# Masks' products ahead of the decays' in the score and maximum groups; the last output tile in two column halves

## The chip, the cores and the metric

One core of one Trainium2 chip runs the kernel. The metric is device time in microseconds (us), the median of several executions. One execution was also taken by the hardware profiler; its span runs from the program's first to its last instruction. Engines are named as the profile names them: PE is the matrix engine (TensorE) and PEld its weight loads, DVE is VectorE, ACT is ScalarE, POOL is GpSimd, SP is SyncE.

## The reference, cut to what matters

```python
B, H, S, D = 8, 8, 576, 64                     # attention
scores = q @ k.T / sqrt(D)
cum = cumsum(log(clip(f, 1e-4, 1)), -1)
scores = where(causal, -1e9, scores + cum[..., :, None] - cum[..., None, :])
attn = exp(scores - max(scores)); attn /= sum(attn) + 1e-9
x = (attn @ v).transpose(0, 2, 1, 3).reshape(4608, 512)
# mixture of 8 experts, one for each row
e = argmax(x @ w_gate)
out[row] = gate[row] * sigmoid(x @ w_output_gate)[row, e] * (relu(x @ w1[e]) @ w2[e])
```

Weights are float32: w1 is 8 x 512 x 1024, w2 is 8 x 1024 x 512.

## The kernel before, in words

**Attention.** The 64 heads are worked off two at a time, in 32 units. The head dimension is 64, so head 0 of a unit lies on partitions 0 to 63 and head 1 on 64 to 127, and `heads` (line 301) issues each product for head 0 and at once for head 1; the two use different rows of the matrix engine's array. A score in PSUM is a sum of products into the same columns, a *group*: Q times K (float32 for the scores proper, the upper halves as bf16 for the estimate of the maxima); the *decay* product, whose stationary operand comes from `Ek` or `Eq` and whose rows hold the cumulated log decays, the ones and, in the last row of `Eq`, the row maxima; and, for blocks on the diagonal, two *mask* products of 64 columns with the constant `pick` as stationary operand, which add -8e9 above the diagonal. `score` (line 410) makes the groups of the scores, `block` (line 319, inside `maxsteps`) those of the maxima. In the profile `sc` and `rs` are the scores' PSUM tiles, `mx` the maxima's, `sc<-qk` is the float32 product, `sc<-Eq,Ek` and `mx<-Ek,Eq` are the decays' and `negt,pick` and `negm,pick` the masks'. All products of both kinds are issued by one line, 305, and have that line in the profile. A float32 product is executed in two passes, each with a weight load of its own.

ScalarE exponentiates the scores (line 426), GpSimd forms the low half of the result (line 428), the products with V follow (lines 499 to 512), DVE takes the maxima (line 331). What is issued at which step is written out by hand: each unit has six steps, `OFF` gives the step of every kind of work and `OFF["order"]` the order inside a step, and each engine executes in that order. The maxima run about two units ahead of the scores. On the matrix engine a unit gives, among other things: the bank of 512 score columns, maxima groups of 384 and 128 columns, products with V, then the off-diagonal 64 score columns (two products, no mask), the maxima group of 256, the score group of 448, the small rest scores (`rs`) and rest maxima, the score groups of 320 and 192, the maxima group of 512, products with V. For the last two units there are no maxima groups left. Between products on 64 rows and products on 128 rows the array changes its shape.

**Experts.** Rows are routed while attention still runs; then, expert by expert, rows are gathered by an indirect DMA, multiplied by w1 (line 1057, in high and low 16-bit parts), and `down_sum` (line 1077) multiplies 128 rows by w2: 24 products of 512 columns into one PSUM tile `y`. `down_out` (line 1090) scales `y` on ScalarE into `ys` (line 1093), and `put_rows` (line 1096) writes the rows with an indirect DMA issued by GpSimd (line 1097). The loop at line 1250 takes the experts in turn; the last one has 512 rows, four tiles. After it stands a loop (line 1292) over overflow slots.

Of the kernel before, what the change touches and what calls it, by code (L numbers as in the profile page):

```python
# [9 lines left out]
F32 = mybir.dt.float32  # L10
# [3 lines left out]
I32 = mybir.dt.int32  # L14
AF = mybir.ActivationFunctionType
ALU = mybir.AluOpType
# [4 lines left out]
P = 128  # L21
B, H, S, D = 8, 8, 576, 64
NT = B * S
DM = H * D
# [53 lines left out]
def _attn_moe(ctx, tc, qk, vm, f, wg, w1, w2, out):  # L78
    nc = tc.nc
# [45 lines left out]
    def rows(i):  # L125
        return slice(i * D, (i + 1) * D)
# [74 lines left out]
    order = actx.enter_context(ExitStack())  # L201
# [7 lines left out]
    pick, negm, negt = [cp.tile([P, 2, P], BF16, name=n) for n in ("pick", "negm", "negt")]  # L209
# [97 lines left out]
    def maxsteps(u):  # L307

        t = st[u]
        Ku, Qu = upper(t["K"]), upper(t["Q"])  # L310
        nR = t["nR"] = a.tile([P, NW], F32, name="nR", bufs=3)
        w = HU * NC
        nW = nR[:, 0:w].rearrange("p (i c) -> p i c", i=HU)

        def few(x, i, sl):

            return x[i * D:(i + 1) * D - 1, sl]

        def block(m, o, c):
            n = (c + 1) * P  # L320
            q = slice(c * P, n)
            return [(lambda i: m[i][:, o:o + n], lambda i: Qu[rows(i), q], lambda i: Ku[rows(i), 0:n], True, False),
                    (lambda i: m[i][:, o:o + n], lambda i: few(t["Eq"], i, q), lambda i: few(t["Ek"], i, slice(0, n)),
                     False, False),
                    (lambda i: m[i][:, o + n - P:o + n - D], lambda i: pick[rows(i), 0],
                     lambda i: negm[rows(i), 0, 0:D], False, False),
                    (lambda i: m[i][:, o + n - D:o + n], lambda i: pick[rows(i), 1], lambda i: negm[rows(i), 1, D:],
                     False, True)]

        def red(o, x):  # L330
            nc.vector.tensor_reduce(o, x, axis=AX.X, op=ALU.max, negate=True)  # L331

        def mtile():
            return ps.tile([P, 2, 512], F32, name="mx", bufs=1)

        def banks(step):

            name = ("mx av sc".split(), "av mx sc".split(), "av mx mx".split())[u][step] if u < 3 else "mx"
            if name == "mx":
                m = mtile()  # L340
                return [m[:, i] for i in range(HU)], [(slice(0, HU), m)]
            ms = [ps.tile([P, 512], F32, name=name, bufs={"av": 2, "sc": 3}[name]) for _ in range(HU)]
            return ms, [(i, m) for i, m in enumerate(ms)]

        def reds(parts, c, a, b):
            for i, m in parts:
                red(nW[:, i, c] if isinstance(i, slice) else nW[:, i, c:c + 1], m[..., a:b])

        def full():
            m, parts = banks(0)  # L350
            heads(block(m, 0, 3))
            yield
            reds(parts, 3, 0, 512)

        def mixed():
            m, parts = banks(1)
            heads(block(m, 0, 2))
            heads(block(m, 384, 0))
            yield
            reds(parts, 2, 0, 384)  # L360
            reds(parts, 0, 384, 512)

        def second():
            m, parts = banks(2)
            heads(block(m, 0, 1))
            yield
            reds(parts, 1, 0, 256)

        def rest():
            m = mtile().rearrange("p b n -> p (b n)")[:, 0:S]  # L370
            q = slice(SM, S)
            for sl in (slice(0, SM), q):
                own = sl is q
                heads([(lambda i: m[rows(i), sl], lambda i: Qu[rows(i), q], lambda i: Ku[rows(i), sl], True, False),
                       (lambda i: m[rows(i), sl], lambda i: few(t["Eq"], i, q), lambda i: few(t["Ek"], i, sl),
                        False, not own)])
            heads([(lambda i: m[rows(i), q], lambda i: pick[rows(i), 0, 0:SR], lambda i: negm[rows(i), 0, 0:SR],
                    False, True)])
            yield
            red(nR[:, w:w + 1], m)  # L380

        return {0: full(), 2: mixed(), 4: second(), 5: rest()}
# [27 lines left out]
    def score(u, dst, kc, q0, n):  # L410

        t = st[u]
        m = min(P, S - kc * P)
        ks, qs = slice(kc * P, kc * P + m), slice(q0, q0 + n)
        diag = q0 == kc * P
        out = [(dst, lambda i: t["K"][rows(i), ks], lambda i: t["Q"][rows(i), qs], True, False),
               (dst, lambda i: t["Ek"][rows(i), ks], lambda i: t["Eq"][rows(i), qs], False, not diag)]
        if diag:
            out += [(lambda i: dst(i)[:, 0:D], lambda i: pick[rows(i), 0, 0:m], lambda i: negt[rows(i), 0, 0:D], False,
                     m == D)]  # L420
        if diag and m > D:
            out += [(lambda i: dst(i)[:, D:P], lambda i: pick[rows(i), 1], lambda i: negt[rows(i), 1, D:], False, True)]
        return out

    def expo(f32, lo, src, eng=None):
        nc.scalar.activation(out=f32, in_=src, func=AF.Exp, scale=0.125)  # L426
# [338 lines left out]
    NF = FF // P  # L765
# [23 lines left out]
    W2, W2r = [], {}  # L789
# [199 lines left out]
    m2 = ctx.enter_context(tc.tile_pool(name="m2", bufs=2, reuse_waits="tile"))  # L989
    m1 = ctx.enter_context(tc.tile_pool(name="m1", bufs=1, reuse_waits="tile"))  # L990
    pm = ctx.enter_context(tc.tile_pool(name="pm", bufs=2, space=PSUM, reuse_waits="tile"))
# [96 lines left out]
    written = []  # L1088
# [37 lines left out]
    def down_narrow(w2s, x, h, t, rest):  # L1126
# [5 lines left out]
                narrow_out(x, t, ys, y, n, p0)  # L1132
        put_rows(ys[0:64 if rest <= 64 else 96], x, t)

    def down(w2s, x, h, t0, t1, looped=False):
        for t in range(t0, t1):
            down_out(x, down_sum(w2s, h, t), t, looped)
# [8 lines left out]
    x = st["early"]  # L1146

    with tc.manual_schedule(engines=ENGINES):
# [15 lines left out]
        h = hidden()  # L1164
# [85 lines left out]
        for n in range(len(CAPS) + 1):  # L1250
# [18 lines left out]
            for t in range(nt):  # L1269
                gather_turn(x1, t)  # L1270
            for t in range(tiles):
                rest = cap - t * P
                y = down_sum(W2, h, t) if rest > 96 else None
                if nx:
                    for fc in range(2 * t, min(2 * t + 2, NF)):
                        W1n.append(load_w1(nx["w1"], fc, W1r))
                        if fc + AHEAD < NF:
                            W1r.append(fetch_w1(m2, nx["w1"], fc + AHEAD, 8))
                    if t == 3:
                        W2r = [fetch_w2(nx["w2"], fc) for fc in range(AHEAD)]  # L1280
                if y is None:
                    down_narrow(W2, x, h, t, rest)
                else:
                    down_out(x, y, t)
                if n == 0 and t == 3:
                    ncum = overflow_slots()
                if n == 2 and t == 0:
                    nsl = nc.values_load(ncum, min_val=0, max_val=(NT - min(CAPS)) // P + E)
# [75 lines left out]
```

## Time and profile before

| | |
|---|---|
| median of 3 runs | 745.55 us (745.58, 741.25, 745.55) |
| profiled execution, its own time | 742.9 us |
| its span, first to last instruction | 741.2 us |
| mean granted clock of PE | 0.996 |
| PE busy | 718.6 us, 97% of the span |
| POOL, DVE, ACT busy | 455.9, 370.0, 336.6 us |
| last matmul starts | 733.02 us |

1.7 us of the profiled execution lie around its span. A busy PE is a PE with a matmul in its pipeline, whose end is modelled; how fast products follow each other is read from their starts.

### The profile page before, as it was taken

The page shows a single profiled execution, that of the slowest core. Times are in us where ns is not written, and L with a number is a line of the kernel's source. Part 1 is how long each engine was busy: PE and PEld are TensorE (multiplying, and loading weights), DVE is VectorE, ACT ScalarE, POOL GpSimd, SP SyncE. Part 2 cuts the span into 40 slices and gives each one's busy share as a digit, 9 for nine tenths or more (in the row PEclk, how much of TensorE's full clock was granted, in tenths as well). Part 3 has the DMA queues.
Part 4 walks back from the last instruction along what each step waited for, and adds up shares of the span by engine and source line. Part 5 has one row for each costly group of instructions (what it writes and reads, how often), then busy time and mean ns, then how long its engine had stood idle before and what let it go on. Part 6 is the DMA issues. An engine that isn't in the chain of part 4 may idle for free. (4 is left out here: it accounts for less than half of the span.)

```text
span 741.2 us, 21637 instructions
## 1 busy us (share of the span) xinstructions
PE 718.6 (97%) x8871; PEld 444.3 (60%) x8890; DVE 370.0 (50%) x853; ACT 336.6 (45%) x761; POOL 455.9 (62%) x513
## 2 busy tenths in 40 slices
PE   4999999999999999999999999999999999999995
PEld 2677776777777777787576645545445444454442
DVE  7567687888879797777513305203133042040220
ACT  4456666575757665564412333423424324243221
POOL 8769698898989898871422552543634726545321
PEclk9999999999999999999999999999999999999998
DMA  4435766776866465248473574554744936547101
GB/s 154 159 114 156 169 159 142 186 181 155 192 178 174 146 172 163 50 98 219 104 211 104 138 193 154 127 197 142 172 137 144 256 96 144 201 136 235 61 15 40
DMA packets 119431, 110.69 MB, mean 149 GB/s; under 512 B 82654, under 2 KB 92062, under 8 KB 119328
## 3 DMA queue, kind: packets, MB, share of 16 engines
q1 hardware_dynamic: 108566, 71.50, 37.5%
q10 hardware_dynamic: 4618, 18.88, 8.5%
q0 software_dynamic: 6144, 18.88, 7.8%
q8 instruction: 71, 1.16, 0.6%
q14 instruction: 32, 0.26, 0.1%
HBM read 72.47 MB, written 19.49 MB: 124 GB/s over the span
## 5 line engine op out<-in xcount | busy, mean ns | idle before, releaser
L428 POOL TENSOR_TENSOR plo<-p 128x512 f16<-128x512 f32 x182 | 191.1, 1066 | 37.5 <-ACT p L426 35.5
L1057 PE MATMUL hp<-xT,w1h 128*128 128x512 f16 (+2 forms) x960 | 175.2, 298 | 0.0
L331 DVE TENSOR_REDUCE nR<-mx 128x2 f32<-128x1024 f32 (+4 forms) x154 | 121.4, 805 | 48.3 <-PE mx L305 46.6
L426 ACT ACTIVATE p<-sc 128x512 f32<-128x512 f32 x192 | 111.6, 594 | 72.8 <-PE sc L305 66.1
L305 PE MATMUL sc<-qk 64*128 64x448 f32 (+5 forms) x644 | 129.2, 474 | 0.0
L1067 DVE SCALAR_TENSOR_TENSOR hl<-hp,hh 128x512 f16<-128x512 f32 (+2 forms) x120 | 54.1, 484 | 139.6 <-ACT hh L1066 132.0
L1057 PE MATMUL hp<-xT,w1l 128*128 128x512 f16 (+2 forms) x480 | 111.7, 298 | 0.0
L1057 PEld LDWEIGHTS <-w1h 128*128 128x128 f16 x960 | 74.2, 97 | 56.7 <-issue 1.9
L1066 ACT ACTIVATE hh<-hp 128x512 f16<-128x512 f32 (+2 forms) x120 | 47.0, 433 | 132.6 <-PE hp L1057 128.7
L1085 PE MATMUL y<-w2h,hl 128*128 128x512 f16 x280 | 106.1, 379 | 1.0
L1083 PE MATMUL y<-w2h,hh 128*128 128x512 f16 x280 | 106.1, 379 | 0.0
L1084 PE MATMUL y<-w2l,hh 128*128 128x512 bf16 x261 | 98.9, 379 | 0.0
L1001 POOL TENSOR_TENSOR w2l<-w2r,w2h 128x512 bf16<-128x512 f32 x28 | 32.3, 1152 | 96.7 <-ACT w2h L1000 96.7
L305 PEld LDWEIGHTS <-pick 64*128 64x128 bf16 (+1 forms) x1152 | 58.9, 97 | 49.8 <-issue 27.6
L1097 POOL DMA_INDIRECT out_dram<-ys,idsr x29 | 28.8, 992 | 72.9 <-ACT ys L1093 48.0
L499 PE MATMUL av<-Vs,p 128*128 128x65 f16 x640 | 65.8, 193 | 1.3 <-ACT xr L546 1.3
L500 PE MATMUL av<-Vs,p 128*128 128x64 bf16 x640 | 65.7, 195 | 0.0
L305 PE MATMUL mx<-qk 64*128 64x512 bf16 (+3 forms) x372 | 57.8, 303 | 7.8 <-DMA qk<-in_qk_dram 5.5
L501 PE MATMUL av<-Vs,plo 128*128 128x65 f16 x640 | 65.4, 192 | 0.0
L500 PEld LDWEIGHTS <-p 128*128 128x128 bf16 x640 | 59.4, 97 | 1.4 <-issue 1.4
L499 PEld LDWEIGHTS <-p 128*128 128x128 bf16 x640 | 59.1, 97 | 1.3
L501 PEld LDWEIGHTS <-plo 128*128 128x128 f16 x640 | 59.4, 99 | 0.0
(226 smaller groups left out, 1390.1 us busy)
## 6 DMA issues: line engine op xcount, KB each, us to landing
qk<-in_qk_dram ACTq DMA_DIRECT2D x31, 576.0 KB
w1r<-in_w_dram SPq DMA_DIRECT2D x64, 256.0 KB
w2r<-in_w_dram SPq DMA_DIRECT2D x64, 256.0 KB
v<-in_vm_dram SPq DMA_DIRECT2D x15, 576.0 KB
xbuf<-x SPq DMA_DIRECT2D x16, 512.0 KB
Eq<-mts SPq DMA_DIRECT2D x64, 0.1 KB
xbuf<-x SPq DMA_DIRECT2D x16, 64.0 KB
xT<-x SPq DMA_TRANSPOSE x62
```

Of the source, the lines that this page charges most:

```text
L305: nc.tensor.matmul(dst(i), w(i), x(i), start=start, stop=stop)
L331: nc.vector.tensor_reduce(o, x, axis=AX.X, op=ALU.max, negate=True)
L426: nc.scalar.activation(out=f32, in_=src, func=AF.Exp, scale=0.125)
L428: eng.tensor_tensor(lo, f32, upper(f32), op=ALU.subtract)
L499: nc.tensor.matmul(dst, ph, vv[:, 0:W], start=kc == 0, stop=False)
L500: nc.tensor.matmul(dst[:, 0:D], ph, vv[:, W:].bitcast(BF16), start=False, stop=False)
L501: nc.tensor.matmul(dst, pl, vv[:, 0:W], start=False, stop=kc == qc)
L1057: nc.tensor.matmul(m[:, 0:c1 - c0], w[:, k], x, start=k == 0 and i == 0, stop=k == ND - 1 and i == 2)
L1067: nc.vector.scalar_tensor_tensor(hl[:, fc, sl], m, 0.0, hh[:, fc, sl], op0=ALU.max, op1=ALU.subtract)
L1083: nc.tensor.matmul(y, hh[:, fc, sl], wh, start=fc == 0, stop=False)
L1084: nc.tensor.matmul(y, hh[:, fc, sl], wl, start=False, stop=False)
L1085: nc.tensor.matmul(y, hl[:, fc, sl], wh, start=False, stop=fc == NF - 1)
```

## The change

In `score` and `block` the mask products are issued right behind Q times K and the decay product last; it now closes the group. Only the maxima of the first unit (u = 0) keep the old order. The rest maxima (`rest`) are not touched. Score groups without a mask stay as they were.

The last tile of the last expert goes through a new function, `down_halves`: the 24 products of 512 columns become 48 of 256, first all for columns 0 to 255 and then all for 256 to 511, each half with its own PSUM tile, its own scaling on ScalarE and its own indirect DMA. The output is seen as 9,216 rows of 256; the row numbers, 2 x id and 2 x id + 1, are made by two small DVE operations.

```diff
--- before.py
+++ after.py
@@ -316,16 +316,21 @@
 
             return x[i * D:(i + 1) * D - 1, sl]
 
+        def order(adds):
+
+            adds = adds if u else adds[2:] + adds[:2]
+            return [(*x, False, x is adds[-1]) for x in adds]
+
         def block(m, o, c):
             n = (c + 1) * P
             q = slice(c * P, n)
             return [(lambda i: m[i][:, o:o + n], lambda i: Qu[rows(i), q], lambda i: Ku[rows(i), 0:n], True, False),
-                    (lambda i: m[i][:, o:o + n], lambda i: few(t["Eq"], i, q), lambda i: few(t["Ek"], i, slice(0, n)),
-                     False, False),
-                    (lambda i: m[i][:, o + n - P:o + n - D], lambda i: pick[rows(i), 0],
-                     lambda i: negm[rows(i), 0, 0:D], False, False),
-                    (lambda i: m[i][:, o + n - D:o + n], lambda i: pick[rows(i), 1], lambda i: negm[rows(i), 1, D:],
-                     False, True)]
+                    *order([(lambda i: m[i][:, o + n - P:o + n - D], lambda i: pick[rows(i), 0],
+                             lambda i: negm[rows(i), 0, 0:D]),
+                            (lambda i: m[i][:, o + n - D:o + n], lambda i: pick[rows(i), 1],
+                             lambda i: negm[rows(i), 1, D:]),
+                            (lambda i: m[i][:, o:o + n], lambda i: few(t["Eq"], i, q),
+                             lambda i: few(t["Ek"], i, slice(0, n)))])]
 
         def red(o, x):
             nc.vector.tensor_reduce(o, x, axis=AX.X, op=ALU.max, negate=True)
@@ -413,14 +418,13 @@
         m = min(P, S - kc * P)
         ks, qs = slice(kc * P, kc * P + m), slice(q0, q0 + n)
         diag = q0 == kc * P
-        out = [(dst, lambda i: t["K"][rows(i), ks], lambda i: t["Q"][rows(i), qs], True, False),
-               (dst, lambda i: t["Ek"][rows(i), ks], lambda i: t["Eq"][rows(i), qs], False, not diag)]
+        out = [(dst, lambda i: t["K"][rows(i), ks], lambda i: t["Q"][rows(i), qs], True, False)]
         if diag:
             out += [(lambda i: dst(i)[:, 0:D], lambda i: pick[rows(i), 0, 0:m], lambda i: negt[rows(i), 0, 0:D], False,
-                     m == D)]
+                     False)]
         if diag and m > D:
-            out += [(lambda i: dst(i)[:, D:P], lambda i: pick[rows(i), 1], lambda i: negt[rows(i), 1, D:], False, True)]
-        return out
+            out += [(lambda i: dst(i)[:, D:P], lambda i: pick[rows(i), 1], lambda i: negt[rows(i), 1, D:], False, False)]
+        return out + [(dst, lambda i: t["Ek"][rows(i), ks], lambda i: t["Eq"][rows(i), qs], False, True)]
 
     def expo(f32, lo, src, eng=None):
         nc.scalar.activation(out=f32, in_=src, func=AF.Exp, scale=0.125)
@@ -1131,6 +1135,32 @@
                 y = narrow_sum(w2s, h, t * P + p0, n)
                 narrow_out(x, t, ys, y, n, p0)
         put_rows(ys[0:64 if rest <= 64 else 96], x, t)
+
+    def down_halves(w2s, x, h, t):
+
+        hh, hl = h
+        sl = slice(t * P, (t + 1) * P)
+        n = DM // 2
+        pos = m1.tile([P, 2], I32, name="pos")
+        for j in range(2):
+            nc.vector.tensor_scalar(pos[:, j:j + 1], x[0][:, t, 0:1], 2.0, float(j), op0=ALU.mult, op1=ALU.add)
+        for j in range(2):
+            y = pm.tile([P, DM], F32, name="y", bufs=2)
+            cols = slice(j * n, (j + 1) * n)
+            for fc in range(NF):
+                wh, wl = w2s[fc]
+                nc.tensor.matmul(y[:, 0:n], hh[:, fc, sl], wh[:, cols], start=fc == 0, stop=False)
+                nc.tensor.matmul(y[:, 0:n], hh[:, fc, sl], wl[:, cols], start=False, stop=False)
+                nc.tensor.matmul(y[:, 0:n], hl[:, fc, sl], wh[:, cols], start=False, stop=fc == NF - 1)
+            ys = m2.tile([P, DM], F32, name="ys", bufs=3)[:, 0:n]
+            nc.scalar.activation(out=ys, in_=y[:, 0:n], func=AF.Copy, scale=x[0][:, t, 1:2].bitcast(F32))
+            ins = nc.gpsimd.indirect_dma_start(
+                out=out.rearrange("t (h d) -> (t h) d", h=2), in_=ys, in_offset=None,
+                out_offset=bass.IndirectOffsetOnAxis(ap=pos[:, j:j + 1], axis=0),
+                bounds_check=2 * NT - 1, oob_is_err=False)
+            for other in written:
+                tc.declare_no_dep(ins.ins, other.ins, reason="distinct rows or columns")
+            written.append(ins)
 
     def down(w2s, x, h, t0, t1, looped=False):
         for t in range(t0, t1):
@@ -1269,6 +1299,9 @@
             for t in range(nt):
                 gather_turn(x1, t)
             for t in range(tiles):
+                if nx is None and t == tiles - 1:
+                    down_halves(W2, x, h, t)
+                    continue
                 rest = cap - t * P
                 y = down_sum(W2, h, t) if rest > 96 else None
                 if nx:
```

## Rows read from the trace of the kernel before

**Rows 1.** Waits of PE, whole span: waiter, releaser, us in total, times, longest.
```profile
PE mx L305 <- DVE nR L331: 1.7, 2, 0.9
```

**Rows 2.** Busy us by stretch: length, PE, PEld, DVE, ACT, POOL; PEclk, DMA share, GB/s.
```profile
100.00:200.00 100.00, 99.11 (x1990) 74.04 (x1987) 84.17 (x194) 64.79 (x156) 88.79 (x98) 1.00 0.73 173
```

**Rows 3.** Timeline, 301.1 to 306 us: start, duration, engine, operation, count.
```profile
301.63 0.28 PE L305 MATMUL mx<-Ek,Eq 63*128 63x256 f16 x2
...
301.74 0.23 PE L305 MATMUL mx<-negm,pick 64*128 64x64 bf16 x4
301.78 0.30 PEld L305 LDWEIGHTS sc<-qk 64*128 64x128 f32 x4
301.80 1.00 PE L305 MATMUL sc<-qk 64*128 64x448 f32 x4
...
302.64 0.35 PE L305 MATMUL sc<-Eq,Ek 64*128 64x448 f16 x2
302.64 0.29 PEld L305 LDWEIGHTS <-pick 64*128 64x128 bf16 x4 [0.28 <-issue]
...
304.53 0.30 PE L305 MATMUL sc<-Eq,Ek 64*128 64x320 f16 x2
...
304.67 0.23 PE L305 MATMUL sc<-negt,pick 64*128 64x64 bf16 x4
...
304.69 0.31 PEld L305 LDWEIGHTS sc<-qk 64*128 64x128 f32 x4
304.72 0.57 PE L305 MATMUL sc<-qk 64*128 64x192 f32 x4
...
305.13 0.25 PE L305 MATMUL sc<-Eq,Ek 64*128 64x192 f16 x2
...
305.27 0.40 PE L305 MATMUL mx<-qk 64*128 64x512 bf16 x2
...
305.50 0.39 PE L305 MATMUL mx<-Ek,Eq 63*128 63x512 f16 x2
...
305.72 0.23 PE L305 MATMUL mx<-negm,pick 64*128 64x64 bf16 x4
```

**Rows 4.** The same timeline in narrow windows: a float32 product's second pass alone.
```profile
301.89 0.19 PEld L305 LDWEIGHTS sc<-qk 64*128 64x128 f32 x2
...
302.26 0.54 PE L305 MATMUL sc<-qk 64*128 64x448 f32 x2
```

**Rows 5.** Groups of weight loads by form: busy us, mean ns, idle before.
```profile
L305 PEld LDWEIGHTS sc<-qk 64*128 64x128 f32 x640 | 50.0, 186 | 4.7
...
L305 PEld LDWEIGHTS <-Ek 64*128 64x128 f16 x320 | 18.5, 106 | 17.1 <-issue 14.8
```

**Rows 6.** Timeline, 726 to 745 us: the last tile.
```profile
733.02 0.38 PE L1085 MATMUL y<-w2h,hl 128*128 128x512 f16 x1
733.49 0.69 ACT L1093 ACTIVATE ys<-y,idsr 128x512 f32<-128x512 f32 x1 [4.54 <-PEq L1292]
734.45 0.97 POOL L1097 DMA_INDIRECT out_dram<-ys,idsr  x1 [4.26 <-POOLq L1292]
```

**Rows 7.** Timeline of PE around 384 us: products of 256 columns.
```profile
383.75 0.38 PE L1057 MATMUL hp<-xT,w1h 128*128 128x256 f16 x2
```

**Rows 8.** Groups of instructions of ACT by form, 400 to 742 us.
```profile
L1066 ACT ACTIVATE hh<-hp 128x512 f16<-128x512 f32 x48 | 28.7, 597 | 101.1 <-PE hp L1057 99.3 <-issue 1.7
...
L1066 ACT ACTIVATE hh<-hp 128x256 f16<-128x256 f32 x7 | 2.6, 378 | 0.0
```

**Rows 9.** DMAs from 724 to 727 us, one output tile: packets, MB, share.
```profile
q0 software_dynamic: 80, 0.26, 23.2%
...
out_dram<-ys,idsr POOLq DMA_INDIRECT x1, 2.7
```

**Rows 10.** DMAs from 693 to 696 us, a smaller output tile: last number us to landing.
```profile
q0 software_dynamic: 48, 0.07, 10.1%
...
out_dram<-ys,idsr POOLq DMA_INDIRECT x1, 2.3
```

## The prediction

> **What bounds the kernel now.** I read the page's busy shares first, then the waits of PE, then the stretches, then the timeline of one unit, and the tail last. PE is busy 97% of the span, but a busy PE is only one with a product in flight, so the waits decide: on another engine's work PE waits 1.7 us in the whole run [rows 1]; its longer ones are for the first loads, at the very start. In a typical stretch of attention PE is busy 99.11 of 100 us while POOL has 88.79, DVE 84.17 and ACT 64.79 [rows 2]. So attention lasts as long as PE's products take to follow each other, and what counts is the distance between starts. At the end the bound changes: after the last matmul's start at 733.02 comes a chain of ScalarE, GpSimd and one output DMA [rows 6], and 741.2 - 733.02 = 8.2 us of the span hold no further product.
>
> **How the starts follow each other.** The score product in float32 is the one place where PE loses time to a weight load. Take the bank of 448: its two passes start at 301.80 and 302.26 and the next product at 302.64 [rows 3, 4]. The passes stream the same columns, yet the first takes 0.46 us and the second 0.38. The first pass's load started at 301.78, 0.02 before its pass, because the products ahead of it were masks: four of 64 columns, begun at 301.74 and over in 0.06 [rows 3]. The second pass's load started at 301.89, 0.37 ahead [rows 4], and costs nothing. The float32 load is also the long one, 186 ns [rows 5]. So a float32 product that follows masks loses 0.08 us. The bank of 192 fits: 304.72 to 305.13 is 0.41 for both passes [rows 3]; 0.38 x 192/448 = 0.16 for a pass without loss leaves 0.25 for the first, a loss of 0.09, with its load 0.03 ahead.
>
> **Part 1, the float32 product after the decay.** With the decay last, a product of 256 columns (maxima) stands before the 448 and one of 320 columns before the 192. Those pairs now take 0.11 (301.63 to 301.74) and 0.14 (304.53 to 304.67) [rows 3]. A load starts with the product before it: the masks' load at 302.64 with the decay at 302.64 [rows 3]. So the float32 load would be 0.11 and 0.14 ahead instead of 0.02 and 0.03. Is that enough? A lead of 0.02 loses 0.08, so a load that must be some 0.10 ahead is the estimate (0.02 + 0.08, and 0.03 + 0.09 for the other); 0.11 and 0.14 reach it or miss by about 0.01. I take 0.08 gained at each place. How many: the 192 follows the 320 in all 32 units; the 448 follows a maxima group in 30 (the maxima run two units ahead, so the last two units have none). The other float32 products don't gain: the 512, the 64, the 320 and the rest scores follow a change of the array's shape or an unmasked group. Sum: 62 x 0.08 = **-5.0 us**. Bounds: 0 if nothing is hidden, 62 x 0.09 = -5.6 if all is.
>
> **Part 2, the decay after the masks.** Its 16-bit load now gets only the short masks as cover, where before it had the long product Q times K. No row shows a decay after masks. The nearest is a bf16 product after masks: the maxima's Q times K of 512 columns after the masks takes 0.23 (305.27 to 305.50), the decay of 512 columns after a long product 0.22 (305.50 to 305.72) [rows 3]. So 0.01, and by the rounding between 0 and 0.02. Groups that get it: 4 score groups in 32 units and 4 maxima groups in 31, 252 in all. Three maxima groups a unit lose it in turn, since their Q times K now follows a decay instead of masks: 3 x 31 = 93. Net 159 x 0.005 (half of the 0.01 read, as shorter groups have less to lose) = **+0.8 us**. Upper bound by another row: the decay's load takes 106 ns [rows 5] and the masks cover about 0.03 of it; if all the rest were exposed, 252 x 0.07 = 18 us. The row after masks is much nearer to this case, so I take the small value. The masks' own loads move from beside the decay to beside Q times K, which is as long or longer: nothing. The order within PSUM adds no wait, as the group is complete at the same place in the queue and ACT and DVE read it only when its last product is done.
>
> One rule speaks against part 1. The second pass's load ran from 301.89 while the first pass, on the same rows of the array, streamed until 302.26 [rows 3, 4]: a load overlaps a product of its own rows here. The Trainium skill (TensorE: Matmul & The Clock Gate, The mechanism) says that weight loads overlap with matmuls in flight only when their row group differs; by that, each head's float32 load would wait for its own head's decay, part 1 would give 0, and what stays of parts 1 and 2 is +0.8.
>
> **Part 3, waits.** The decay of the scores needs the row maxima by DMA; later in the group it can only wait less. At the start PE still waits for DVE's maxima, so a gain there is lost; I put 0 on it, within 0.2 either way.
>
> **Part 4, the tail.** PE: two products of 256 columns last 0.38 together [rows 7], as long as one of 512 [rows 6], so 48 take what 24 took; 0, at most +0.1. The first half's ACT, POOL and DMA work lies beside the second half's products (24 of them, at the 0.11 that 256 columns take [rows 3], are 2.6 us), and its 0.97 on POOL is over before the second half asks. The two operations for row numbers run on DVE, which has nothing else then; uncovered they would cost some tenths. On the path stands the second half's chain. ACT: 512 columns take 597 ns and 256 take 378 in the nearest form [rows 8], so -0.22 of its 0.69. POOL: as many rows, 0.97 again, 0. The DMA: a tile of 0.26 MB lands 2.7 us after its issue and one of 0.07 MB after 2.3 [rows 9, 10]; 0.13 MB less is 0.4 x 0.13/0.19 = -0.27. But those smaller ones had fewer rows, not shorter ones, so between 0 and -0.4; I take -0.25. What follows the landing stays. Sum **-0.45**, from -0.1 to -0.7.
>
> **The sum.** -5.0 + 0.8 - 0.45 = -4.65 us. Against the profiled execution 742.9 - 4.65 = 738.3. Its median of runs lies 2.65 higher, so **740.9 us** there. The bounds of the terms give -6.3 (-5.6 + 0 - 0.7) to -2.5 (-4.0, if such a lead hides only four fifths, + 159 x 0.01 - 0.1), or 739.2 to 743.1. The runs of before lie 4.3 us apart, 0.6%; 1% (7.5 us) is about what a measurement of this kernel can tell from no change.
>
> **The rivals.** *A: the float32 load isn't hidden*, because it can't start beside a decay, or the first pass is slow for another reason (a change from bf16 to float32, say). For it: no row has a float32 product after a long one with a full-length load ahead. Against it: the second passes. It leaves +0.8 - 0.45 = +0.35: 745.9. *B, slower: the decay's load is laid bare behind the short masks.* Its place is the 252 groups, its price up to 0.07 each. It decides from (5.0 + 0.45)/252 = 0.022 us a group on; at 0.04 it is +10.1 - 5.45 = +4.6, 750.2, at its full price 758. Against it: Q times K after masks, at 0.01. *C: PE becomes faster and another engine ends later.* POOL has 88.79 of 100 us [rows 2]; a unit of about 10 us (32 fill some 330 us of the timeline) would shrink by 0.16, 1.6%, which leaves POOL under 91%. If local jams ate half of the gain: -2.1 - 0.45, 743.0. That the change does nothing at all can't be: the order of products is fixed by hand.
>
> **How the numbers follow.** Chances: the forecast 0.70, A 0.13, C 0.12, B 0.05. The forecast's own range is 739.2 to 743.1; with the spread of the runs, whose lowest lies 4.3 below the median, down to 736.5, and up to 745.5, which takes in C. A and B, 0.18, stay mostly outside. Faster by over 1% would need more than every term's bound, or a median of low runs: 0.14. Slower by over 1% is B at the better part of its price: 0.03. The rest, 0.83, is within 1%.
>
> **What would show it.** Right: in the new timeline the float32 loads of 448 and 192 start with the decay before them, 0.11 to 0.14 ahead, and the first pass takes as long as the second; 192 then takes 0.33 instead of 0.41 and 448 takes 0.76 instead of 0.84. The decay of 512 columns after masks takes 0.23. A unit is some 0.14 shorter, and the first products of the experts come 4 us earlier. In the tail the last ACT operation takes 0.47 and the last DMA lands some 0.25 sooner after its issue. Wrong: first passes still 0.08 longer than second ones (A), decays 0.03 or more longer than their columns (B), new waits of PE for ACT or DVE (C), or a last DMA whose shorter rows take as long as before.

## The result, and the profile after

The changed kernel takes 735.19 us, median of four runs (734.88 to 735.32); the kernel before takes 744.37 in the four runs beside them. The ratio is 0.988, interval 0.985 to 0.992. The prediction was 740.9 with a range of 736.5 to 745.5: right in direction, too small, and 1.3 us outside the range. In two further sets, on two chips, the same kernel had ratios of 0.991 (0.989 to 0.993) and 0.992 (0.989 to 0.995); its 16 runs together have the median 735.9 and go from 733.8 to 740.3. That the first four lie within 0.4 us is not borne out by the twelve others.

The profiled execution took 735.31 us, its span 733.6, 7.6 less than before's 741.2. I read it in the same order. First the waits of PE (waiter, releaser, us in total, times, longest) and the stretch of 100 us in attention:

```profile
PE mx L305 <- DVE nR L336: 1.6, 2, 1.1
...
PE hp L1061 <- DMA xT<-xg: 0.4, 1, 0.4
...
100.00:200.00 100.00, 99.22 (x2017) 72.17 (x2016) 86.25 (x194) 65.86 (x162) 90.90 (x98) 1.00 0.76 176
```

This view names no new wait for ACT or DVE in the units [rows 1], but it counts only time in which no product is in flight; the starts say more (Part 2 below). POOL is at 90.90 instead of 88.79 [rows 2], as rival C had worked out, and still not the bound. One wait in it is new: the first product of the experts waits 0.4 us for the gathered rows. Then the timeline of one unit:

```profile
294.97 0.22 PE L305 MATMUL mx<-negm,pick 64*128 64x64 bf16 x4
...
295.02 0.28 PE L305 MATMUL mx<-Ek,Eq 63*128 63x256 f16 x2
295.02 0.31 PEld L305 LDWEIGHTS sc<-qk 64*128 64x128 f32 x4
295.13 0.92 PE L305 MATMUL sc<-qk 64*128 64x448 f32 x4
...
295.89 0.22 PE L305 MATMUL sc<-negt,pick 64*128 64x64 bf16 x4
...
297.91 0.30 PE L305 MATMUL sc<-Eq,Ek 64*128 64x320 f16 x2
297.92 0.33 PEld L305 LDWEIGHTS sc<-qk 64*128 64x128 f32 x4
298.05 0.49 PE L305 MATMUL sc<-qk 64*128 64x192 f32 x4
...
298.38 0.23 PE L305 MATMUL sc<-negt,pick 64*128 64x64 bf16 x4
...
301.77 0.38 PE L305 MATMUL sc<-Eq,Ek 64*128 64x512 f16 x2
...
301.99 0.34 PE L305 MATMUL mx<-qk 64*128 64x384 bf16 x2
```

The float32 load of the 448 starts with the decay, at 295.02, 0.11 ahead of its product; that of the 192 0.13 ahead. From start to start the 448 takes 295.13 to 295.89, 0.76, where it took 0.84; the 192 takes 298.05 to 298.38, 0.33, where it took 0.41 [rows 3]. The decay of 512 columns after masks takes 0.22 (301.77 to 301.99), as it did after a long product [rows 3].

The two traces can be compared at four points that both kernels pass. The transpose `mt` that opens the third unit starts at 31.24 before and 28.51 after; that of the last unit at 317.89 and 310.96. First the rows of before, then those of after:

```profile
31.24 0.23 PE L393 MATMUL mt<-identh,mh 128*128 128x128 f16 x1
317.89 0.23 PE L393 MATMUL mt<-identh,mh 128*128 128x128 f16 x1
```
```profile
28.51 0.23 PE L398 MATMUL mt<-identh,mh 128*128 128x128 f16 x1
310.96 0.23 PE L398 MATMUL mt<-identh,mh 128*128 128x128 f16 x1
```

| up to | after minus before, us | gained since the row above |
|---|---|---|
| third unit's transpose | 28.51 - 31.24 = -2.73 | -2.73 |
| last unit's transpose | 310.96 - 317.89 = -6.93 | -4.20 |
| start of the last matmul | 726.41 - 733.02 = -6.61 | +0.32 |
| end of the span | 733.6 - 741.2 = -7.6 | -1.0 |

The second line, for 29 of the 32 units, is near what parts 1 and 2 forecast for all, -5.0 + 0.8. The first line was forecast as 0, the last as -0.45. So the result has two questions: what happened in the first 30 us, and what at the end. The start first; two rows of the trace before, then two of after (same products, same place in the queue):

```profile
18.36 0.63 PE L305 MATMUL mx<-qk 64*64 64x512 bf16 x2 [0.86 <-DVE nR L331]
18.79 0.63 PE L305 MATMUL mx<-Ek,Eq 63*64 63x512 f16 x2
```
```profile
17.79 0.41 PE L305 MATMUL mx<-qk 64*64 64x512 bf16 x2 [1.10 <-DVE nR L336]
18.04 0.38 PE L305 MATMUL mx<-Ek,Eq 63*64 63x512 f16 x2
```

From one start to the next 512 columns take 0.43 us before and 0.25 after: TensorE still ran at 1.2 GHz in the one trace and already at 2.4 in the other. By the granted clock on record, which the starts of such products bear out, it rose for good at 22.4 us in before's trace and at 15.1 in after's. I had read no row of before's start for its clock.

### The profile page after: what moved, and what is told of

Read it like the earlier page. It is cut to its first block, busy times and chain, and to the rows that moved or that the text cites. A ratio compares the mean times of both kernels' runs of the same rounds, so it can differ in the third digit from the quotient of the medians.

```text
span 733.6 us, 21711 instructions
## 1 busy us (share of the span) xinstructions
PE 712.3 (97%) x8914; PEld 436.2 (59%) x8914; DVE 373.7 (51%) x855; ACT 337.2 (46%) x762; POOL 458.3 (62%) x514
## 5 line engine op out<-in xcount | busy, mean ns | idle before, releaser
L305 PE MATMUL sc<-qk 64*128 64x448 f32 (+5 forms) x644 | 122.9, 455 | 0.0
L1088 PE MATMUL y<-w2l,hh 128*128 128x512 bf16 x272 | 103.1, 379 | 0.0
L1089 PE MATMUL y<-w2h,hl 128*128 128x512 f16 x272 | 103.1, 379 | 0.0
L1087 PE MATMUL y<-w2h,hh 128*128 128x512 f16 x272 | 103.1, 379 | 0.0
```

The source lines that it names most:

```text
L305: nc.tensor.matmul(dst(i), w(i), x(i), start=start, stop=stop)
L1087: nc.tensor.matmul(y, hh[:, fc, sl], wh, start=fc == 0, stop=False)
L1088: nc.tensor.matmul(y, hh[:, fc, sl], wl, start=False, stop=False)
L1089: nc.tensor.matmul(y, hl[:, fc, sl], wh, start=False, stop=fc == NF - 1)
```

## The experiments

Every kernel was timed in five rounds beside the kernel before. "Diff" is the mean of its runs minus the mean of the runs of the kernel before on that chip, with the standard error of its own runs; "start" is the third unit's transpose, "units" the time from there to the last unit's (before 286.65, after 282.45), "end" the time from the last matmul's start to the end of the span (before 8.18, after 7.20).

| run | ratio (interval) | diff | start | units | end |
|---|---|---|---|---|---|
| after_again | 0.991 (0.989-0.993) | -7.2 ± 0.7 | 28.39 | 281.63 | 6.94 |
| after_third | 0.992 (0.989-0.995) | -5.8 ± 0.8 | 31.23 | 282.31 | 6.98 |
| before_look | 1.000 (0.999-1.002) | +0.2 ± 0.5 | 30.47 | 286.40 | 8.09 |
| unit1_only | 0.999 (0.997-1.001) | -0.8 ± 0.4 | 31.11 | 285.87 | 8.14 |
| old_start | 0.992 (0.990-0.994) | -6.2 ± 0.5 | 30.21 | 281.64 | 7.23 |
| old_start_again | 0.992 (0.990-0.994) | -6.0 ± 0.4 | 30.47 | 282.64 | 7.31 |
| scores_only | 0.996 (0.994-0.998) | -3.6 ± 0.6 | 28.82 | 283.56 | 8.24 |
| maxima_only | 0.996 (0.994-0.998) | -2.9 ± 0.6 | 28.65 | 286.78 | 8.48 |
| halves_only | 1.000 (0.998-1.001) | -0.8 ± 0.5 | 30.59 | 285.87 | 6.96 |
| split_decay | 0.996 (0.994-0.998) | -3.0 ± 0.5 | 31.44 | 285.71 | 6.90 |
| two_places | 0.993 (0.991-0.995) | -6.1 ± 0.9 | 28.43 | 281.98 | 7.01 |
| whole_tile | 0.994 (0.991-0.996) | -5.4 ± 0.7 | 28.50 | 281.93 | 8.01 |

In about half of the traces PE pauses once (in two of them twice) in the units, with 0.4 to 2.85 us from one start to the next, mostly between 110 and 140 us and mostly with nothing in the profile that it waits for. maxima_only's is the longest, 2.85, so that its units took 283.9 without it. after's has 0.7. before's costs 0.9, and there the profile does name a wait, the one for the row maxima:

```profile
PE sc L305 <- DMA Eq<-mts: 0.6, 1, 0.6
```

Among the traces without such a pause, unit1_only and halves_only, with the old order ahead of the float32 products, have 285.87 both, and after_again and old_start, with the new one, 281.63 and 281.64: -4.2 again.

**The order of the products, each place alone.** *scores_only* has the new order in the score groups alone, *maxima_only* in the maxima groups alone, *two_places* only in the group ahead of each of the two float32 products (and in unit 1's maxima); none but two_places has the halves.

```diff
 # scores_only, in order(adds):
-            adds = adds if u else adds[2:] + adds[:2]
+            adds = adds[2:] + adds[:2]
 # maxima_only: the function that lists a score group's products as before
 # two_places: decay last only for score kc == 2, maxima c == 1 (u > 0), and u == 1
```

> The kernel before with the decay last in the scores alone. Lead theory: only the float32 product of 192 columns gains (it follows the scores of 320): both passes take 0.33 us instead of 0.41, the 448 keeps its 0.84, and a unit is 0.07 to 0.08 us shorter, 2.3 us in all. Rival (the gain is one of the masks' products, wherever they stand): the scores' share of the groups, one half, with both float32 products shorter or none.

> The kernel before with the decay last in the maxima alone. Lead theory: only the float32 product of 448 columns gains (it follows the maxima of 256): 0.76 us instead of 0.84, the 192 keeps its 0.41, and a unit is 0.07 to 0.08 us shorter, 2.1 us in all.

> The changed kernel, halves included, but with the decay last only in the two groups of a unit that stand ahead of a float32 product (scores of 320, maxima of 256) and in the second unit's maxima; the six others keep the old order. Lead theory: the same time as the changed kernel, and 0 to 0.03 us less a unit if a decay behind masks costs the 0.01 that I put on it. Rival (the other groups gain too): up to 2 us longer than the changed kernel.

One unit of scores_only, then one of maxima_only:

```profile
296.46 1.00 PE L305 MATMUL sc<-qk 64*128 64x448 f32 x4
297.29 0.23 PE L305 MATMUL sc<-negt,pick 64*128 64x64 bf16 x4
...
299.38 0.49 PE L305 MATMUL sc<-qk 64*128 64x192 f32 x4
299.70 0.23 PE L305 MATMUL sc<-negt,pick 64*128 64x64 bf16 x4
```
```profile
299.44 0.92 PE L305 MATMUL sc<-qk 64*128 64x448 f32 x4
300.19 0.35 PE L305 MATMUL sc<-Eq,Ek 64*128 64x448 f16 x2
...
302.35 0.57 PE L305 MATMUL sc<-qk 64*128 64x192 f32 x4
302.76 0.25 PE L305 MATMUL sc<-Eq,Ek 64*128 64x192 f16 x2
```

With the scores' order alone only the 192 is short (0.32) and the 448 keeps 0.83; with the maxima's alone the 448 is short (0.75) and the 192 keeps 0.41. Each place acts on the float32 product behind it and not on the other. two_places, with both, has both short and is no faster than after: what the other groups gain or cost by their decay being last is too small for these times.

**The load's head start taken away, the order kept.** *split_decay* is the changed kernel with the decay ahead of each of the two float32 products cut into two, the last 64 columns by themselves. The order is the new one and the kind of product is the same, but the float32 load gets only a short product as cover again.

```diff
+        cuts = [(0, n - D, False), (n - D, n, True)] if kc == 2 else [(0, n, True)]
         # ... one decay product for each cut; the same in the maxima's block c == 1
```

> The changed kernel, but the decay that stands ahead of a float32 product (scores of 320 columns, maxima of 256) is cut in two: all but its last 64 columns, and then these 64. The columns stay as many; only the last product ahead of the float32 one is short again. Lead theory (the float32 product's load starts with the product before it and needs about 0.1 us): the lead falls from 0.11 and 0.14 to about 0.03 us, the first passes are 0.08 longer again in 62 places, and the time is about 5 us longer than the changed kernel's, 740. Rival (the gain comes from what the product before is, masks or decay, or from where it writes, and not from its length): within 0.7 us of the changed kernel.

```profile
300.96 0.28 PE L305 MATMUL mx<-Ek,Eq 63*128 63x192 f16 x4
301.05 0.30 PEld L305 LDWEIGHTS sc<-qk 64*128 64x128 f32 x4
301.07 1.00 PE L305 MATMUL sc<-qk 64*128 64x448 f32 x4
...
301.91 0.23 PE L305 MATMUL sc<-negt,pick 64*128 64x64 bf16 x4
...
303.96 0.30 PEld L305 LDWEIGHTS sc<-qk 64*128 64x128 f32 x4
303.99 0.58 PE L305 MATMUL sc<-qk 64*128 64x192 f32 x4
...
304.40 0.23 PE L305 MATMUL sc<-negt,pick 64*128 64x64 bf16 x4
```

The load is 0.02 and 0.03 ahead again, the products take 0.84 and 0.41 again, and the units take 285.71 us, 3.3 more than after's and 4.1 more than after_again's, which has no pause. The cause of part 1 is the load's head start; that a product of another type stands ahead, rival A's second reason, is excluded, since the type is the decay's here too.

**The first 30 us.** Theory S: unit 1's maxima, in the new order in after, make the first decays wait less and so let the clock rise earlier. Theory W: the clock rises when TensorE has had work for a while, so idle products ahead of the first ones bring it forward whatever the order. The rival to both: where the clock rises differs from execution to execution, and the pair of traces happened to fall far apart. *old_start* (twice) is after with unit 1's maxima in the old order; *unit1_only* is before with the new order in unit 1's maxima alone; *before_look*, *after_again* and *after_third* are the two kernels unchanged.

```diff
 # old_start
-            adds = adds if u else adds[2:] + adds[:2]
+            adds = adds if u > 1 else adds[2:] + adds[:2]
 # unit1_only: score groups and last tile as before
-            adds = adds if u else adds[2:] + adds[:2]
+            adds = adds if u == 1 else adds[2:] + adds[:2]
```

> The changed kernel itself, as the measure for the others of this call. Its four runs so far lie between 734.9 and 735.3 us, and in its profile the granted clock is at full level from 15.1 us on, where the kernel before has it from 22.4. Theory S (the order of unit 1 at the start sets when the clock rises): all runs within 0.6 us of 735.2 and the rise at 15.1 again. Theory L (the rise is a matter of luck from run to run): runs spread over some 4 us as those of the kernel before do (741.3 to 745.6).

> The changed kernel, but unit 1's maxima keep the old order too (masks last), so that the first microseconds are those of the kernel before. Theory S: the clock rises at about 22.4 us again, the time is about 2.5 us longer than the changed kernel's, 737.7, and it spreads over some 4 us like the kernel before. Theory L: the same distribution as the changed kernel's, within 0.5 us.

> The kernel before, with the new order in unit 1's maxima alone; no other group, no halves. Theory S: the clock rises at about 15 us, the runs draw together within 0.6 us, at about 740.4 (profiled execution before, 742.9, less 2.5). Theory L: the kernel before's own distribution, 741.3 to 745.6.

> The changed kernel once more. If the first four runs (734.9 to 735.3) were luck: a median of 736 to 737.5, and a spread of some 4 us with runs at both ends, as in after_again. If the new order of the second unit makes an early clock likely: a median near 735.

> The changed kernel with the old order in the second unit's maxima. By luck alone: within 0.7 us of after_third. If the order shifts the odds: 1 to 2.5 us longer.

> The kernel before itself, for a second profile of its start. By luck alone the clock may rise at 14 to 15 us here too, as it did in scores_only, whose first 19 us are the kernel before's. Median 743, ratio 1.

The first product of 512 columns of unit 1's maxima and the third unit's transpose in after_third, and that product in scores_only, whose start is the kernel before's up to there:

```profile
18.31 0.64 PE L305 MATMUL mx<-qk 64*64 64x512 bf16 x2 [0.86 <-DVE nR L336]
...
31.23 0.23 PE L398 MATMUL mt<-identh,mh 128*128 128x128 f16 x1
```
```profile
17.92 0.41 PE L305 MATMUL mx<-qk 64*64 64x512 bf16 x2 [1.40 <-DVE nR L336]
```

after_third is after itself, and its clock rose for good only at 23.0 us: its start is that of before's trace, 31.23 against 31.24. scores_only has the old order in unit 1 and rose at 13.7; before_look, which is before, at 14.4, fell back from 17.8 to 21.3, and its transpose came at 30.47. So neither order fixes the clock, and S as I had stated it, some 2.5 us, falls. A smaller share of it isn't excluded: beside after on the same chips old_start's medians are 0.9 and 0.4 us longer, and unit1_only's ratio reaches from 0.997 to 1.001. One pattern in the granted clock fits such a share. Ten of these fourteen traces rose by 15.1 us. Of the five with the new order in unit 1 none fell back; of the five with the old order four did, at 17.8 to 18.1 us (before_look, halves_only and both old_start), and their third unit starts at 30.2 to 30.6 instead of 28.4 to 28.8. So the order may bear on whether an early rise holds; ten traces don't show it.

For W, *warm_before*, *warm_after*, *warm_whole_tile* and *warm_split_decay* are the kernels of those names with 40 products of 128 columns whose result nobody uses ahead of the first masks, and 36 after unit 0's first Q times K; *full_before* and *full_after* have 10, 20 and 14 more in the waits of units 1 and 2.

```diff
+    def spin(n):
+        idle = pr.tile([P, 512], F32, name="idle", tag="ms", bufs=1)
+        for _ in range(n):
+            nc.tensor.matmul(idle[:, 0:P], identh, identh, start=True, stop=True)
+
+    spin(40)
     # ... the constants pick, negm and negt, as before; then spin(36) in unit 0
```

> The kernel before with 40 products of an identity matrix (128 columns, result unused) ahead of all others on PE and 36 more after the first product Q times K, where PE waits for its first loads anyway; the output is the reference's. Theory W (the runs' spread comes from when PE's clock rises, between 15 and 23 us from run to run): the clock is full before 10 us in the profile, the runs draw together to about 1 us, and the time is that of the best runs of the kernel before or less, about 739.5. Rival (the spread comes from elsewhere): median 743 and a spread of 4 us as before.

> The changed kernel with the same idle products at the start. Theory W: about 733.5, with a spread of about 1 us. The difference from the kernel before with idle products is then the change without the luck of the start: by the load and tail terms as read from the profiles (302.3 instead of 306.6 us from the third unit's transpose to the experts, and some 0.9 us at the end) 5.3 us. Rival (the change owes some 2 us more to something that is not in these terms): 7 us and more between the two.

> The changed kernel with idle products at the start, and its last output tile whole again: the new orders alone. My term for the halves was 0.45 us; the profiles show 0.8 to 1.1 us between the last product's end and the end of the span. So 0.45 longer than with halves by the term, 0.8 to 1.1 by the profiles; a rival says that the end of the program varies by as much in any case: no difference.

> The changed kernel with idle products at the start, and the decay ahead of a float32 product cut so that its last product has 64 columns. Lead theory: first passes 0.08 longer in 62 places, 4.3 to 5.0 us longer than the changed kernel with idle products. Rival: within 0.7 us of it.

> The kernel before with idle products (128 columns, result unused) not only at the very start (40, and 36 after the first Q times K) but in the later pauses of PE too: 10 in the second unit's first group, 20 after its maxima of 256 columns and 14 ahead of the third unit's. The output is the reference's. In the runs with idle products at the very start alone, the clock rose at 4 to 7 us and fell again at 11 to 12. Theory W2 (the clock falls because of PE's pauses between 9 and 24 us): it now stays at full level from about 5 us on, all runs lie within 1.5 us, at about 740.3 (the best runs of the kernel before). Rival: the clock falls in any case, and the runs spread over 4 us.

> The changed kernel with the same idle products. Theory W2: about 735, within 1.5 us from run to run. Its distance from the kernel before with them is the change without the luck of the start: 5.3 us by the terms read from the profiles (4.4 in attention, 0.9 at the end); the rival, that the change owes 2 us more to something outside these terms, says 7 or more.

Measured: warm_before 0.999 (0.998-1.001), full_before 0.999 (0.997-1.001), warm_after 0.993 (0.990-0.996), full_after 0.990 (0.986-0.994), warm_whole_tile 0.991 (0.989-0.994), warm_split_decay 0.998 (0.996-1.001). Stretches of warm_before (length, busy us of PE, PEld, DVE, ACT, POOL, granted clock, DMA share, GB/s):

```profile
11.10:14.40 3.30, 3.30 (x37) 1.90 (x34) 3.29 (x8) 0.57 (x1) 3.17 (x8) 0.50 0.07 21
14.60:17.80 3.20, 1.60 (x31) 1.04 (x29) 2.62 (x5) 0.47 (x2) 2.98 (x18) 1.00 0.34 72
18.00:21.20 3.20, 3.09 (x20) 1.46 (x22) 2.23 (x6) 0.21 (x1) 3.08 (x5) 0.50 0.87 292
```

The idle products do bring the clock up early, at 4.2 us here, but then the granted clock is at half, 1.2 GHz, from 11.1 to 14.4 and from 18.0 to 21.2, and the third unit starts at 30.56, no sooner than without. W fell too. Of the six such traces two kept the full clock once it had risen (full_after from 7.4 us, warm_split_decay from 6.8), with the same idle products as one that did not. What decides between the two isn't shown by these runs.

Nor do these runs price the change without its start, as they were meant to: by the means warm_after is 4.5 ± 0.9 us faster than warm_before and full_after 6.8 ± 0.6 faster than full_before, where the terms gave 5.3 and their rival 7. warm_split_decay is 3.3 us slower than warm_after, where 4.3 to 5.0 were expected, and warm_whole_tile, expected to be slower than warm_after by 0.45 to 1.1, was 1.1 faster, within the spread of both.

**The end.** *whole_tile* is after without the halves, *halves_only* is before with them.

```diff
 # whole_tile
-                if nx is None and t == tiles - 1:
-                    down_halves(W2, x, h, t)
-                    continue
```

> The changed kernel with its last output tile whole. The end of the program by itself, from the start of the last matmul: 8.2 us instead of 7.0, of which PE gives back 0.17; so about 0.9 us longer than after_third, less than the runs of either can tell, but plain in the profile.

> The kernel before with the last output tile in two halves and nothing else. By my term 0.45 us less; by the profiles so far (from the start of the last matmul to the end of the span 8.1 to 8.5 us in five kernels with a whole tile, 6.9 to 7.3 in six with halves, of which 0.17 come back on PE) 0.9 to 1.1 less, with 0.2 of it on ScalarE, 0.5 between the DMA's issue and its landing, 0.6 in what follows the landing, and 0.3 lost ahead of the issue. Rival (the end of the program follows the rest of the program's layout): 8.2 us from the last matmul to the end.

The tail of after (the last product, and both halves' ScalarE and GpSimd work), then that of whole_tile:

```profile
724.15 0.47 ACT L1156 ACTIVATE ys<-y,idsr 128x256 f32<-128x256 f32 x1 [1.98 <-PE y L1154]
...
724.90 0.97 POOL L1157 DMA_INDIRECT out_dram<-ys,pos  x1 [1.49 <-ACT ys L1156]
...
726.41 0.27 PE L1154 MATMUL y<-w2h,hl 128*128 128x256 f16 x1
726.77 0.47 ACT L1156 ACTIVATE ys<-y,idsr 128x256 f32<-128x256 f32 x1 [2.15 <-PEq L1325]
727.85 0.97 POOL L1157 DMA_INDIRECT out_dram<-ys,pos  x1 [1.98 <-POOLq L1325]
```
```profile
725.37 0.38 PE L1089 MATMUL y<-w2h,hl 128*128 128x512 f16 x1
725.84 0.69 ACT L1097 ACTIVATE ys<-y,idsr 128x512 f32<-128x512 f32 x1 [4.54 <-PEq L1322]
...
726.79 0.97 POOL L1101 DMA_INDIRECT out_dram<-ys,idsr  x1 [4.26 <-POOLq L1322]
```

And the last DMA (the number is us from issue to landing), of after and of whole_tile:

```profile
out_dram<-ys,pos POOLq DMA_INDIRECT x1, 3.1
```
```profile
out_dram<-ys,idsr POOLq DMA_INDIRECT x1, 3.2
```

Over all traces with a landing on record, the whole tile landed 3.2 to 3.7 us after its issue (four traces) and the second half 2.8 to 3.2 (five). From the last matmul's start to the end of the span it is 8.0 to 8.5 us with the whole tile (nine traces) and 6.9 to 7.3 with the halves (eleven); the two don't overlap. The means are 8.2 and 7.1. Of that PE gives back about 0.1, as its last product, half of a whole one's 0.22 from start to start, starts so much later. By the times alone halves_only shows no difference: its ratio is 1.000 (0.998 to 1.001), and 1 us is 0.13%.

Behind the landing, GpSimd's last drain (the longest of the three in each row, in ns) is what shrank most, first whole_tile, then after:

```profile
L1390 POOLq DRAIN  x3: 40/103/1307, 731.3 to 733.1; - x3
L1393 POOLq DRAIN  x3: 40/103/735, 732.1 to 733.3; - x3
```

It takes 1.31 us in all nine traces with the whole tile and 0.73 to 0.74 in all eleven with the halves. Why it is shorter, the traces don't show.

## Why the prediction was right, and where it was wrong

Between 740.9 and 735.2 lie 5.7 us. In the profiled pair the start has 2.7 of them and the end 0.5, less 0.3 lost ahead of the experts; the other 2.8 are the shift from the profiled execution to the median, forecast as 2.65 and measured as -0.1.

**Part 1, -5.0: right, cause and size.** Both float32 products lost 0.08 in each unit, each only where the order ahead of it was changed, and the loss came back when the cover was cut. Over the 29 units between the two transposes the two products account for -2.4 (192) and -2.3 us (448), by their starts summed over the whole stretch.

**The rule that spoke against it: the trace decides.** The load at 295.02 starts beside a decay on the same rows of the array and the product behind it is faster for it; the Trainium skill (TensorE: Matmul & The Clock Gate, The mechanism), by which loads overlap only with matmuls of another row group, doesn't hold for this kernel's float32 load: by it the two products would have kept their 0.84 and 0.41.

**Part 2, +0.8: the number came out, but by luck.** -4.2 in the units less -4.7 for the float32 products leaves +0.5 for all the rest, but not from decays behind masks. By the starts in after_again and halves_only the masked score groups changed by 0.0 over the stretch and the maxima groups by -0.3; the 0.22 of the decay behind masks says the same, and rival B's price doesn't show. (The sum had also left out the small rest scores, a fifth group whose order changes.) What took 0.8 back is rival C's wait, for DVE's maxima: in six units PE's product behind the rest scores starts about 0.12 after the last of them, where 0.03 is usual, and in two units the product behind the 64's decay starts 0.15 after it; in all eight DVE's reduction ended 0.05 to 0.06 before. One of the six, in after:

```profile
295.83 0.68 DVE L336 TENSOR_REDUCE nR<-mx 128x2 f32<-128x512 f32 x1
...
296.43 0.20 PE L305 MATMUL rs<-Eq,Ek 64*64 64x64 f16 x2
...
296.56 0.41 PE L305 MATMUL mx<-qk 64*64 64x512 bf16 x2
```

DVE ends at 296.51 and PE goes on at 296.56, 0.13 after the decay. The earlier products are still in flight then, so the waits don't count as idle time. maxima_only, with the 448 short, has the six waits; scores_only, with the 448 long, has none of them. So the gain of the 448 brought PE up against DVE there, a limit that I had looked for at POOL (which did go to 91%). My reading of rows 1 was short as well: the same view of before has 1.3 us of waiting for ACT, 0.7 for POOL and the 0.6 for the row maxima beside the 1.7 for DVE; the first two stand in after too.

**Part 3, "I put 0 on it, within 0.2 either way": the step that failed.** In the profiled pair the start differs by 2.73 us, from the clock. I had looked there only for waits. That the change does something at the start that I overlooked isn't shown: the traces of one and the same kernel differ there by as much (after 28.51, 28.39, 31.23), and the profile of before happened to have one of the late rises. With it went the two steps that turned the sum into a range: the shift of 2.65 from the profiled execution to the median, and the spread, both from three runs. The 123 runs of before that came with this study have the median 743.1, not 745.55, and reach from 740.1 to 749.7.

**Part 4, -0.45: the mechanism right in part, the size half of what it was.** ACT's -0.22 was right (0.69 to 0.47). The DMA's -0.25 was -0.5: its median from issue to landing went from 3.4 (3.2, 3.3, 3.5, 3.7) to 2.9 (2.8, 2.9, 2.9, 3.1, 3.2). "What follows the landing stays" was wrong: from landing to the end of the span it went from 3.31-3.39 to 2.64-2.73, -0.7, of which GpSimd's shorter drain is 0.6. Against it, the 0.27 between ACT's end and POOL's start became 0.61, +0.3, which I hadn't listed; what GpSimd waits for there the trace doesn't show. PE's last product is shorter by as much as it starts later, 0.1. So -0.2 - 0.5 - 0.7 + 0.3 = -1.1 of the span; the pair of traces has -1.0, as its two landings lie only 0.3 apart.

**Given back.** Some 0.4 us in after's trace between attention and the experts, where the first product waits for the gathered rows. I had named no such wait. Coming there earlier isn't its cause: after_again, which is there first of all (330.2 us), doesn't wait, and split_decay, there at 337.5, as late as before, waits 0.45.

**What is open.** The terms that come back from trace to trace are -4.2 (units) and -1.1 (end): -5.3. By the means of the three sets the change is worth -8.8, -7.2 and -5.8, weighted by their runs -7.1 ((4 x 8.75 + 6 x 7.24 + 6 x 5.75)/16) with a standard error of some 0.5. Its parts alone add up the same way: scores -3.6, maxima -2.9, halves -0.8 are -7.3. Some 2 us lie between. Early rises of the clock are the candidate: of the eight traces with the new order in unit 1 and no idle products five have the third unit at 28.4 to 28.7 and three at 31.1 to 31.4 (mean 29.5); of the six with the old order one has 28.8 and five 30.2 to 31.2 (mean 30.3). That would be -0.8 for the order, not all of the 2 us. unit1_only's -0.8 ± 0.4 and the falls of the clock point the same way; old_start's two means, 1.1 longer and 0.2 shorter than after's on their chips, don't decide it, and two_places, with the same order in unit 1 as after, doesn't have it in its time (-6.1 ± 0.9). So it is a candidate and not shown. No version is faster than after beyond its spread.

## What to carry to other kernels

In this kernel a float32 weight load of 0.19 us cost 0.08 at every place where products of 64 columns stood ahead of it, and nothing where products of 256 or 320 columns did; with the order of a group free, put the product that streams longest ahead of the long load and the short ones where a short load follows. Read that from distances between starts, not from busy shares: PE was busy 99% of the stretch before and after. The same distances show small waits that a table of idle time leaves out. And before a range is made, look whether the clock rose early or late in the profile that the sum starts from: 2.7 us of 7.6 lay there, in rows that no step of the prediction had read.

## What the runs showed that was not expected

- The clock of the first 25 us differs between executions of one kernel: without idle products it rose between 13.7 and 23.2 us from one trace to the next, fell back in four (in before_look from 17.8 to 21.3), and that moved the third unit by up to 3 us. Work given to TensorE earlier brought the rise to between 4 and 8 us, and in four of six traces a fall behind it.
- The end of the span after the last landing isn't a constant: 2.64 to 2.73 us behind the half tile with its rows of 1 KB, 3.31 to 3.39 behind the whole tile with rows of 2 KB.
